# A gated linear attention with routed experts on one core: scaled states on ScalarE, a second load of values, and a shorter routing sequence

## The chip, the core and the metric

The kernel runs on one core of a Trainium2 chip. The core has five engines that work side by side, each through its own list of instructions and in that list's order: TensorE (PE in the profile, with its weight loads shown as PEld), VectorE (DVE), ScalarE (ACT), GpSimd (POOL) and SyncE (SP). SP here only issues DMAs; ACT and POOL issue some as well. The metric is the device time of one execution in microseconds, as the median of several runs. Lower is better.

## What is computed

A decayed linear attention over 4 batches, 8 heads, 768 tokens and head size 48, and behind it a mixture of 8 experts with one expert for each token:

```python
for t in range(S):
    state = alpha[:, :, t, :, None] * state + np.einsum('bhd,bhe->bhde', k[:, :, t], v[:, :, t])
    y[:, :, t] = np.einsum('bhd,bhde->bhe', q[:, :, t], state)
...
        fresh_e = int(np.argmax(logits[b, s]))
        if s == 0 or local_gate[b, s] < 0.5:
            e = fresh_e
        else:
            e = prev_e if prev_e >= 0 else fresh_e
        prev_e = e
...
        h = np.maximum(x[b, s] @ w1[e], 0.0)
        out[b, s] = p[e] * (h @ w2[e])
```

The attention's output of one token (8 heads of 48, that is 384 numbers) is the expert layer's input x. The expert of a token depends on the tokens before it, since a closed local gate takes over the expert of its predecessor. The hidden size of an expert is 1024. Everything is in float32; the expert matmuls split each operand into a high and a low part (`hi`, `lo`) and add three products.

## The kernel before

**The attention loop.** The 3072 tokens are 24 blocks of 128 tokens (`NB`), and block i belongs to batch i % 4, so four independent states take turns. The loop at L684 has 26 passes, called slots here; in slot i the steps of neighbouring blocks are interleaved. From L658 on (`pinned[0] = True`) the program order of each engine is kept, so that order decides who stands behind whom. One slot i issues, in this order:

- `one_a(i+2)` (a small memset on POOL) and `scan2(i+1)`: the backward scan `sf` on DVE, then the product of k with it on POOL.
- `kt(i)`: four transposes on PE into `kp`, copied by ACT to `kk`.
- `copies(i-1)`: two copies on ACT of the states into `sb`. `state(i-1)`: the scaled state with which the batch's next block begins, one operation on DVE.
- `pm(i)`: 32 small matmuls into `pe`, masked by DVE to `pq`.
- up to three of the one-time preparations in `made` (L660), most of them on POOL.
- `other()`, the first of three places a slot. Each place lets every routing sequence go one step, and then either issues matmuls of zeros (`dense`, two a place, so six a slot) or, once the experts have begun, one piece of expert work. The first place of a slot gives no piece before slot 24.
- `scan1(i+2)`: the forward scan `A` and a reciprocal on DVE, then the product of q with `A` on POOL. Loads of block i+3 on SP.
- `xt(i-2)`: three transposes of the finished rows; after each fourth block a routing sequence is added (slots 5, 9, 13, 17, 21 and 25).
- `ym(i-1)`: 48 matmuls into `y`, of which the last 16 read `sb`; ACT copies them to `XR` and stores them to `xd`. A load of values on SP.
- `first_v(i+1)`: ACT copies the first 64 rows of the values beside themselves, since the update wants them in a form of their own.
- the second place; `um(i)`: 16 matmuls into `up`, and DVE adds the state (`st`); the third place.

**The routing.** `route(g)` (L432) finds for four blocks the expert and the place of each token. It is a generator: each `yield` ends a step, and a step is issued at a place. Before, it has 16 steps (13 for the last group): logits `lg`, transposes `lt`, the argmax chain ending in `kr`, an empty step, `rp`, the scan `em`, `rb`, the counts `oi`, the probability, `pw`, the places ending in `oa`, then the value rows `vo` (POOL) and the one-hot rows `on` (ScalarE, two operations for each of the four blocks, spread over four steps; the last group has both on DVE), and eight matmuls `lp` on PE whose sum DVE adds to `acc`. `acc` is the list from which tokens are gathered.

**The early experts.** When the routing of the first 12 blocks ends (`T1`), `work[0] = early()` (L562) begins: it gathers the tokens of expert 0, waits out four more places, and then yields pieces: two transposes (`tp`), eight `h` pieces of the first matrix (`gemm1`, nine matmuls each), eight pieces of the second, then the same for expert 1. The PSUM buffer `tr` is one and is shared by `kp`, `xp` and `tp`; the buffer for all routing results is one as well (`RT`). After the loop, routing 5 is run out place by place, one piece each; then the rest of the experts follow at L738 and L753.

**Start.** Before the order is pinned, POOL clears constants and work buffers (L269 to L280 and L647 to L655), and the first blocks are loaded by `load_a`, `load_x` and `load_v`, nine DMAs on SP's queue.

Of the kernel before, what the change touches and what calls it, by code (L numbers as in the profile page):

```python
# [45 lines left out]
DN0 = 32  # L46
DN = 2
HL = ("h", "h", "up", "pe")
# [18 lines left out]
def gla_moe(ctx, tc, akq, vw, vn, wg, w1, w2, cst, tok, out):  # L67
# [45 lines left out]
    def cc(k, p0=0, p1=128):  # L113
        a, b = _off[k]
        return cs[p0:p1, a:b]
# [140 lines left out]
    with ExitStack() as ac, ExitStack() as aa:  # L256
# [16 lines left out]
        for j in range(2):  # L273
            sb = ap.tile([R, 2, 2, CW], F32, bufs=1, name=f"sb{j}")
            g_.memset(sb[0:64], 0.0)
            g_.memset(sb[64:112, :, 1, :], 0.0)
            SBs.append(sb)
            oh = ap.tile([128, E, G + 1], F32, bufs=1, name=f"oh{j}")
            g_.memset(oh, 0.0)
            OHs.append(oh)  # L280

# [29 lines left out]
        def load_v(i):  # L311
            at = i % G * NBB + i // G
            y_.dma_start(VTs[i % NP][:, 1, :], vn[:, at * DM:(at + 1) * DM])

        def first_v(i):
            vt = VTs[i % NP]
            s_.copy(vt[0:64, 0, :], vt[0:64, 1, :])

        def scan1(i):

            d = blk[i]
            x, a = d["x"], d["a"]
            A = ap.tile([R, SW], F32, tag="A", bufs=3, name=f"A_{i}")
            v_.tensor_tensor_scan(A, a[:, 0:SW], z1, 0.0, ALU.mult, ALU.add)
            d["end"] = A[:, 2 * C + 1:SW:2 * (C + 1)]
            v_.reciprocal(z2[0:R, 2 * C + 1:SW:2 * (C + 1)], d["end"])
            q2 = x[:, BW:].rearrange("p (s t) -> p s t", t=C)
            g_.tensor_tensor(q2, q2, A.rearrange("p (s t) -> p s t", t=C + 1)[:, :, 1:], ALU.mult)
            d["k"] = x[:, 0:BW].rearrange("p (h t) -> p h t", h=HP)
            d["q"] = x[:, BW:2 * BW].rearrange("p (h t) -> p h t", h=HP)  # L330

        def one_a(i):
            a = blk[i]["a"]
            g_.memset(a[:, C + 1:SW:2 * (C + 1)], 1.0)
# [60 lines left out]
        def state(i):  # L395
            d = blk[i]
            if i + G < NB:
                sn = ap.tile([R, 3, HP, D], F32, tag="st", bufs=G + 1, name=f"st_{i + G}")
                v_.scalar_tensor_tensor(sn[:, 0], d["s3"][:, 2], 1.0 / SEED,
                                        d["end"].unsqueeze(2).broadcast_to([R, HP, D]), ALU.mult, ALU.mult)  # L400
                st["S", i % G] = sn
# [30 lines left out]
        def route(g):  # L432
# [4 lines left out]
            def rt(shape, nm, dt=F32, bufs=2):  # L437
                return ap.tile(shape, dt, tag=nm, bufs=bufs, name=f"{nm}_{g}")
# [29 lines left out]
            yield  # L468
            yield

# [27 lines left out]
            v_.reciprocal(se, se)  # L498
            yield
            v_.tensor_tensor(ex, ex, ob, ALU.mult)  # L500
            pn = rt([128, n], "pn")
            v_.tensor_reduce(pn, ex, AX.X, ALU.add)
            v_.tensor_tensor(pl[:, :, 0], pn, se, ALU.mult)
            yield
# [3 lines left out]
            t_.matmul(pw[:, :, 0:n], lhsT=trif, rhs=o4, start=False, stop=True)  # L508
            yield
            ps = rt([128, E, n + 1], "ps")  # L510
            v_.tensor_tensor(ps, pw, st["c"].unsqueeze(2).broadcast_to([128, E, n + 1]), ALU.add)
# [23 lines left out]
            on = ap.tile([128, n, TS], F32, bufs=1, tag="on", name=f"on_{g}")  # L535
            if end:
                v_.tensor_tensor(on, iob.unsqueeze(1).broadcast_to([128, n, TS]),
                                 rr.unsqueeze(2).broadcast_to([128, n, TS]), ALU.is_equal)
            else:
                for j in range(n):  # L540
                    s_.activation(on[:, j], iob, AF.Abs, bias=rr[:, j:j + 1], scale=-1.0)
                    s_.activation(on[:, j], on[:, j], AF.Relu, bias=one[:, 0:1], scale=-float(TS))
                    if j < n - 1:
                        yield
            yield
# [16 lines left out]
        def early():  # L562
# [8 lines left out]
            for _ in jobs[0].gather():  # L571
                yield False
            for _ in range(4):
                yield False
            for _ in jobs[0].trans():
# [45 lines left out]

        def other(pieces=True):

            flush()
            for r in list(steps):
                if next(r, 0) == 0:
                    steps.remove(r)
            if work[0] is None:
                if DN:
                    dense(DN)  # L630
            else:
                if last and drained[0]:
                    last[0].ht, last[0].yt = HL, YL
                for done in work[0] if pieces else ():
                    if done or steps or not drained[0]:
                        break

        work, drained = [None], [False]
        for i in range(3):
# [7 lines left out]
        g_.memset(one, 1.0)  # L647
        g_.memset(m5, 1.0)
        g_.memset(m5[:, :, 0], 0.0)
        for e in range(E):  # L650
            g_.memset(c0[:, e:e + 1], float(e * RS - 1))
            g_.memset(c1[:, e:e + 1], float(e * RS - 1 + (C1 if e in EARLY else 0)))
        g_.tensor_copy(trif, cc("tri"))
        g_.memset(trif[0:64, 64:128], 1.0)
        g_.memset(trif[64:128, 0:64], 0.0)  # L655
        nc.scalar.dma_start(xd[0:1], z2[127:128, 0:DM])
        first_v(0)
        pinned[0] = True  # L658
        dense(DN0)
        made = [  # L660
            lambda: g_.memset(fill, 0.0),
            lambda: g_.tensor_copy(fill.bitcast(I32)[:, 1:2], tk[0:SL, 2 * NB:]),
# [12 lines left out]
                                     -float(SENT), None, ALU.add),  # L675
            lambda: g_.tensor_copy(vals[:, :, 2], tk[:, 1:2 * NB:2]),
        ]
        one_a(0)
        scan1(0)
        scan2(0)  # L680
        one_a(1)
        scan1(1)
        wsteps = iter(())
        for i in range(NB + 2):  # L684
# [16 lines left out]
            other(i >= NB)  # L701
            if i + 2 < NB:
# [238 lines left out]
```

## Time and profile before

| what | value |
|---|---|
| three runs | 488.93, 488.33, 485.93 us; median 488.33 us |
| the profiled execution, its own time | 484.0 us |
| its span, first to last instruction | 482.2 us |
| mean granted TensorE clock over the span | 0.961 |
| HBM read and written | 55.84 MB and 10.62 MB |
| blocks 1 to 22 of the attention loop, from mask `pq` to mask | 20.59 to 153.57 us |

In the profile a row of the groups gives the line, engine, operation, the output and its inputs by the program's names, the shape, the count, then busy microseconds and the mean nanoseconds of one. As a helper records every operation, all have line L81; tiles tell them apart. A row of a timeline begins with its start and its duration in microseconds, and where the engine had been idle before it, the idle time and what ended it stand in brackets. A row of the windows gives the length of a stretch and then the busy time of each engine, the granted clock as a share of full speed, and the DMA engines' share and rate.

### The profile page before, as it was taken

The numbers are of one execution on the slowest core, as the hardware profiler recorded it, in microseconds if no ns is written. First come the engines' busy times: TensorE is split into PE (matmuls) and PEld (weight loads), VectorE is DVE, ScalarE is ACT, GpSimd is POOL, SyncE is SP. The second block draws the span as 40 slices with busy tenths as digits, with TensorE's granted clock in tenths as the row PEclk, the third lists the DMA queues.
The fourth block names the chain that finished last, engine by engine and source line by source line (L and its number), as shares of the span: only waits on it lengthen the run. The fifth ranks groups of instructions, "written<-read, shape, count | busy, mean of one in ns | idle before, by whom it ended". The sixth has DMA issues, their size and how long they took to land.

```text
span 482.2 us, 10873 instructions
## 1 busy us (share of the span) xinstructions
PE 437.9 (91%) x4443; PEld 391.5 (81%) x4443; DVE 257.3 (53%) x485; ACT 194.1 (40%) x390; POOL 186.7 (39%) x207
## 2 busy tenths in 40 slices
PE   5999898999997978698989999999999999999990
PEld 5777776878875877597878998998989989989990
DVE  4778999898997235722274445244254252342310
ACT  1345656565756436321354324335144233242210
POOL 6654326364556000261053642724732503504201
PEclk9799999999998899888899999999999999999997
DMA  8789767596661102660075554444351542531100
GB/s 217 199 260 252 222 187 201 164 292 167 189 208 50 51 17 71 180 186 27 1 224 188 134 181 138 124 131 123 114 175 57 158 130 65 174 98 39 50 3 27
DMA packets 26710, 66.01 MB, mean 137 GB/s; under 512 B 4384, under 2 KB 10677, under 8 KB 26658
## 3 DMA queue, kind: packets, MB, share of 16 engines
q1 hardware_dynamic: 18672, 49.65, 36.3%
q0 software_dynamic: 3840, 10.62, 6.9%
q10 hardware_dynamic: 4146, 5.03, 3.1%
q8 instruction: 35, 0.57, 0.5%
q14 instruction: 17, 0.14, 0.1%
HBM read 55.84 MB, written 10.62 MB: 138 GB/s over the span
## 4 chain that ended last, share of the span: by engine, by line
PE 53%; issue 11%; DVE 9%; ACT 3%; POOL 2%; POOLq 0%; DVEq 0%; ACTq 0%
PE h L81 24%; PE yp L81 20%; PE y L81 3%; PE tp L81 2%; DVE A L81 2%; POOL out L81 1%; PE up L81 1%; DVE st L81 1%; DVE sf L81 1%; DVE pq L81 1%; ACT hh L81 1%; POOL w1l_0b L81 1%; PE pe L81 1%; DVE xl L81 1%; PE lp L81 1%
## 5 line engine op out<-in xcount | busy, mean ns | idle before, releaser
L81 DVE SCALAR_TENSOR_TENSOR hl<-h,hh 128x480 fp32r<-128x480 f32 (+2 forms) x80 | 43.9, 556 | 77.2 <-ACT hh L81 76.9
L81 ACT ACTIVATE hh<-h 128x480 fp32r<-128x480 f32 (+2 forms) x80 | 38.7, 490 | 82.4 <-PE h L81 82.3
L81 POOL DMA_INDIRECT out<-yo,idx x32 | 32.5, 1017 | 80.5 <-DVE yo L81 78.0
L81 POOL DMA_INDIRECT xg<-xd,idx x32 | 32.6, 1018 | 61.0 <-PE tp L81 52.9
L81 DVE TENSOR_SCALAR yo<-yp,acc 128x384 f32<-128x384 f32 (+1 forms) x32 | 19.6, 616 | 61.1 <-PE yp L81 61.0
L81 POOL TENSOR_TENSOR x<-x,sf 112x512 f32<-112x512 f32 x24 | 29.0, 1209 | 42.5 <-DVE sf L81 42.5
L81 POOL TENSOR_TENSOR x<-x,A 112x512 f32<-112x512 f32 x24 | 31.8, 1327 | 29.0 <-DVE A L81 6.6
L81 DVE TENSOR_TENSOR_SCAN A<-a,z 112x520 f32<-112x520 f32 x24 | 34.5, 1437 | 5.6 <-POOL a L81 5.6
L81 PE MATMUL h<-dz 128*128 128x256 f32 x142 | 35.0, 354 | 2.1 <-DVE z L81 2.1
L81 DVE TENSOR_TENSOR_SCAN sf<-a,z 112x520 f32<-112x520 f32 x24 | 33.8, 1408 | 0.1
L81 ACT COPY sb<-st 48x384 f32<-48x384 f32 x48 | 24.5, 510 | 11.5 <-DVE st L81 10.9
L81 PEld LDWEIGHTS h<-dz 128*128 128x128 f32 x142 | 23.8, 224 | 6.5 <-DVE z L81 2.1
L81 PEld LDWEIGHTS y<-vt,pq 64*64 64x64 f32 x768 | 24.9, 138 | 4.0 <-issue 3.8
L81 PE MATMUL y<-vt,pq 64*64 64x48 f32 x768 | 27.9, 224 | 0.0
L81 PE MATMUL y<-sb,x 112*64 112x96 f32 x384 | 21.8, 258 | 4.3 <-ACT sb L81 4.2
L81 PE MATMUL up<-vt,kk 128*48 128x96 f32 (+1 forms) x384 | 23.1, 267 | 0.0
L81 PEld LDWEIGHTS y<-sb,x 112*64 112x64 f32 x384 | 17.2, 140 | 6.2 <-ACT sb L81 5.2
L81 PEld LDWEIGHTS up<-vt,kk 128*48 128x48 f32 (+1 forms) x384 | 18.3, 140 | 3.4 <-issue 1.0
L81 ACT COPY kk<-kp 128x448 f32<-128x448 f32 x24 | 12.8, 531 | 20.7 <-PE kp L81 20.6
L81 PE MATMUL h<-xh,w1h_1a 128*128 128x256 f32 (+1 forms) x48 | 16.4, 342 | 3.9 <-DVE hl L81 2.7
L81 ACT COPY XR<-y 128x384 f32<-128x384 f32 x24 | 11.5, 479 | 20.1 <-PE y L81 20.1
L81 ACT CAST xh<-tp 128x384 fp32r<-128x384 f32 (+1 forms) x32 | 14.0, 462 | 13.9 <-PE tp L81 13.6
(247 smaller groups left out, 1234.8 us busy)
## 6 DMA issues: line engine op xcount, KB each, us to landing
x<-akq SPq DMA_DIRECT2D x24, 448.0 KB, 5.6
a<-akq SPq DMA_DIRECT2D x24, 227.9 KB, 4.5
vt<-vn SPq DMA_DIRECT2D x24, 192.0 KB, 2.7
xd<-XR ACTq DMA_DIRECT2D x24, 192.0 KB, 4.8
rw_0a<-w SPq DMA_DIRECT2D x3, 512.0 KB, 4.9
rw_0a<-w SPq DMA_DIRECT2D x4, 384.0 KB, 4.2
rw_1a<-w SPq DMA_DIRECT2D x3, 512.0 KB, 5.9
rw_1a<-w SPq DMA_DIRECT2D x4, 384.0 KB, 3.5
```

What stands on the lines that cost most here:

```text
L81: r = f(*a, **k)
```

## The change

Nothing changes in the arithmetic's result; what changes is where and when parts are done.

- The next state (`state`) is made by four ScalarE activations with a scale for each partition, in place of one DVE operation. The scale `dec` is made on POOL in `scan1`. In a slot, `kt(i)` now stands behind `copies(i-1)` and `state(i-1)`, so ScalarE copies `kk` after these.
- `first_v` goes; `load_v` issues a second DMA of 96 KB that loads the first 64 rows again.
- `on` is one DVE comparison for all groups. The product of the probability goes from DVE to POOL (`eo`).
- The routing has 11 steps: the empty step and the three in which `on` was spread are gone, two others are joined, so that `vo` and `on` stand at one place and `lp` at the next. `early()` waits out two places, not four.
- Matmuls of zeros: two at a slot's first place, one at each of the others, four a slot.
- POOL clears less ahead of the loop: one-time memsets move into `made`, of which up to five a slot are issued; `c0` and `c1` are worked out by two DVE operations, a copy and two memsets. The first product of q (`scale_q(0)`) stands behind the first `scan2`.

```diff
-DN = 2
+DN = 1
@@ buffers
-            g_.memset(sb[0:64], 0.0)
-            g_.memset(sb[64:112, :, 1, :], 0.0)
+            if j == 0:
+                g_.memset(sb[0:64], 0.0)
+                g_.memset(sb[64:112, :, 1, :], 0.0)
...
-            g_.memset(oh, 0.0)
@@ load_v
             y_.dma_start(VTs[i % NP][:, 1, :], vn[:, at * DM:(at + 1) * DM])
-
-        def first_v(i):
-            vt = VTs[i % NP]
-            s_.copy(vt[0:64, 0, :], vt[0:64, 1, :])
+            y_.dma_start(VTs[i % NP][0:64, 0, :], vn[0:64, at * DM:(at + 1) * DM])
@@ scan1
-            q2 = x[:, BW:].rearrange("p (s t) -> p s t", t=C)
-            g_.tensor_tensor(q2, q2, A.rearrange("p (s t) -> p s t", t=C + 1)[:, :, 1:], ALU.mult)
+            d["A"] = A
+            if i + G < NB:
+                d["dec"] = ap.tile([R, HP], F32, tag="dec", bufs=4, name=f"dec_{i}")
+                g_.tensor_scalar(d["dec"], d["end"], 1.0 / SEED, None, ALU.mult)
+            if i:
+                scale_q(i)
...
+        def scale_q(i):
+            q2 = blk[i]["x"][:, BW:].rearrange("p (s t) -> p s t", t=C)
+            g_.tensor_tensor(q2, q2, blk[i].pop("A").rearrange("p (s t) -> p s t", t=C + 1)[:, :, 1:], ALU.mult)
@@ state
-                v_.scalar_tensor_tensor(sn[:, 0], d["s3"][:, 2], 1.0 / SEED,
-                                        d["end"].unsqueeze(2).broadcast_to([R, HP, D]), ALU.mult, ALU.mult)
+                for hp in range(HP):
+                    s_.activation(sn[:, 0, hp], d["s3"][:, 2, hp], AF.Copy, scale=d["dec"][:, hp:hp + 1])
@@ route
             yield
-            yield
...
-            yield
-            v_.tensor_tensor(ex, ex, ob, ALU.mult)
-            pn = rt([128, n], "pn")
-            v_.tensor_reduce(pn, ex, AX.X, ALU.add)
-            v_.tensor_tensor(pl[:, :, 0], pn, se, ALU.mult)
+            eo = rt([128, n, 8], "eo")
+            g_.tensor_tensor(eo, ex, ob, ALU.mult)
             yield
             pw = pp.tile([128, E, n + 1], F32, tag=RT, name=f"pw_{g}")
...
             yield
+            pn = rt([128, n], "pn")
+            v_.tensor_reduce(pn, eo, AX.X, ALU.add)
+            v_.tensor_tensor(pl[:, :, 0], pn, se, ALU.mult)
...
-            if end:
-                v_.tensor_tensor(on, iob.unsqueeze(1).broadcast_to([128, n, TS]),
-                                 rr.unsqueeze(2).broadcast_to([128, n, TS]), ALU.is_equal)
-            else:
-                for j in range(n):
-                    s_.activation(on[:, j], iob, AF.Abs, bias=rr[:, j:j + 1], scale=-1.0)
-                    s_.activation(on[:, j], on[:, j], AF.Relu, bias=one[:, 0:1], scale=-float(TS))
-                    if j < n - 1:
-                        yield
+            v_.tensor_tensor(on, iob.unsqueeze(1).broadcast_to([128, n, TS]),
+                                              rr.unsqueeze(2).broadcast_to([128, n, TS]), ALU.is_equal)
             yield
@@ early
-            for _ in range(4):
-                yield False
+            yield False
+            yield False
@@ other
-                if DN:
-                    dense(DN)
+                dense(dn)
@@ before the loop
         made = [
+            lambda: g_.memset(SBs[1][0:64], 0.0),
+            lambda: g_.memset(SBs[1][64:112, :, 1, :], 0.0),
+            lambda: g_.memset(one, 1.0),
+            lambda: g_.memset(OHs[0], 0.0),
+            lambda: g_.memset(OHs[1], 0.0),
+            lambda: g_.memset(m5, 1.0),
+            lambda: g_.memset(m5[:, :, 0], 0.0),
+            lambda: g_.tensor_copy(trif, cc("tri")),
...
         one_a(0)
         scan1(0)
         scan2(0)
+        scale_q(0)
@@ a slot
-            if i < NB:
-                kt(i)
             if 0 < i <= NB:
                 copies(i - 1)
                 state(i - 1)
             if i < NB:
+                kt(i)
+            if i < NB:
                 pm(i)
...
-            for _ in range(min(3, len(made))):
+            for _ in range(min(5, len(made))):
                 made.pop(0)()
-            other(i >= NB)
+            other(i >= NB, 2)
...
-            if i + 1 < NB:
-                first_v(i + 1)
```

More of the change, by code (lines that the diff above doesn't have):

```diff
@@ L274, in gla_moe @@
             sb = ap.tile([R, 2, 2, CW], F32, bufs=1, name=f"sb{j}")
-            g_.memset(sb[0:64], 0.0)
-            g_.memset(sb[64:112, :, 1, :], 0.0)
+            if j == 0:
+                g_.memset(sb[0:64], 0.0)
+                g_.memset(sb[64:112, :, 1, :], 0.0)
             SBs.append(sb)
-            oh = ap.tile([128, E, G + 1], F32, bufs=1, name=f"oh{j}")
-            g_.memset(oh, 0.0)
-            OHs.append(oh)
+            OHs.append(ap.tile([128, E, G + 1], F32, bufs=1, name=f"oh{j}"))
         st = {"c": c0}
@@ L620, in gla_moe, with other @@
         last, EW, steps = [], {}, []
-        def other(pieces=True):
+        def other(pieces=True, dn=DN):
             flush()
@@ L646, in gla_moe @@
                 nc.scalar.dma_start(wgs, wg[:, :, 0:32])
[L647 to L655, printed above, removed]
         nc.scalar.dma_start(xd[0:1], z2[127:128, 0:DM])
-        first_v(0)
         pinned[0] = True
@@ L660, in gla_moe @@
         made = [
+            lambda: g_.memset(SBs[1][0:64], 0.0),
[6 more added lines that the diff above has]
+            lambda: g_.tensor_copy(trif, cc("tri")),
+            lambda: g_.memset(trif[0:64, 64:128], 1.0),
+            lambda: g_.memset(trif[64:128, 0:64], 0.0),
             lambda: g_.memset(fill, 0.0),
@@ L676, in gla_moe @@
             lambda: g_.tensor_copy(vals[:, :, 2], tk[:, 1:2 * NB:2]),
+            lambda: v_.tensor_scalar(c0, ioa[:, :, 0], WH, float(TS), ALU.subtract, ALU.mult),
+            lambda: v_.tensor_scalar(c0, c0, -1.0, None, ALU.add),
+            lambda: g_.tensor_copy(c1, c0),
+        ] + [
+            lambda e=e: g_.memset(c1[:, e:e + 1], float(e * RS - 1 + C1)) for e in EARLY
         ]
```

## The prediction

> **What bounds the kernel now.** First the page: the busy shares of the engines.
>
> ```profile
> PE 437.9 (91%) x4443; PEld 391.5 (81%) x4443; DVE 257.3 (53%) x485; ACT 194.1 (40%) x390; POOL 186.7 (39%) x207
> ```
>
> TensorE is busy for 91%, but an average hides the stages. So next the windows, cut at the ends of `up` in slots 5, 11, 15, 19, then at the end of slot 23, at the end of the third `h` piece of expert 1 (208), and the rest (from a second call).
>
> ```profile
> core 0: us, PE busy (x) PEld busy (x) DVE busy (x) ACT busy (x) POOL busy (x), PEclk, DMA share, GB/s
> 22.50:46.50 24.00, 22.33 (x461) 18.66 (x460) 18.38 (x29) 12.54 (x26) 12.81 (x19) 1.00 0.86 249
> 46.50:88.70 42.20, 37.30 (x699) 31.23 (x699) 38.45 (x74) 25.94 (x60) 18.16 (x21) 0.96 0.65 192
> 88.70:113.90 25.20, 24.42 (x477) 20.50 (x477) 22.72 (x48) 15.89 (x40) 12.41 (x13) 1.00 0.78 237
> 113.90:137.00 23.10, 22.73 (x468) 19.26 (x468) 21.78 (x48) 14.75 (x38) 12.62 (x16) 1.00 0.70 193
> 137.00:171.20 34.20, 29.08 (x485) 24.00 (x485) 20.43 (x50) 16.92 (x42) 11.84 (x11) 0.90 0.28 82
> 171.20:208.00 36.80, 28.81 (x234) 25.88 (x235) 20.15 (x59) 15.80 (x35) 6.97 (x7) 0.92 0.38 113
> 250.00:460.00 210.00, 209.20 (x1133) 193.15 (x1132) 82.80 (x128) 73.48 (x118) 82.65 (x57) 1.00 0.41 123
> ```
>
> From 250 on TensorE has no gap (209.20 of 210.00), and the change touches nothing there: what is won or lost earlier is carried to the end. Slots 6 to 11 are bounded by VectorE (38.45 of 42.20, it also splits expert 0's weights), slots 12 to 19 by TensorE (24.42 of 25.20 and 22.73 of 23.10) with VectorE close behind. In the last two stages nobody is full: TensorE idles 5.1 and 8.0 us, and its clock is 0.90 and 0.92, while pieces wait for their places. That idle time is what a shorter routing can win.
>
> **The change part by part.** The sum goes by these stages. First the rows for the loop.
>
> ```profile
> 108.67 0.55 PE L81 MATMUL kp<-cs,x 112*128 112x112 f32 x4
> ...
> 112.58 0.50 PE L81 MATMUL h<-dz 128*128 128x256 f32 x2
> 113.01 0.88 PE L81 MATMUL up<-vt,kk 128*48 128x96 f32 x16
> 113.82 0.51 PE L81 MATMUL h<-dz 128*128 128x256 f32 x2
> 114.17 0.55 PE L81 MATMUL kp<-cs,x 112*128 112x112 f32 x4
> ```
>
> ```profile
> L81 PE MATMUL h<-dz 128*128 128x256 f32 x142 | 35.0, 354 | 2.1 <-DVE z L81 2.1
> L81 DVE SCALAR_TENSOR_TENSOR st<-st,A 112x192 f32<-112x192 f32 x20 | 7.6, 378 | 0.0
> L81 DVE TENSOR_TENSOR on<-iob,rr 128x512 f32<-128x512 f32 x1 | 0.7, 684 | 0.0
> L81 ACT COPY vt<-vt 64x384 f32<-64x384 f32 x24 | 12.3, 512 | 12.3 <-ACT XR L81 8.5 <-DMA vt<-vn 3.9
> L81 ACT ACTIVATE on<-on,one 128x128 f32<-128x128 f32 x20 | 8.0, 402 | 0.6
> L81 ACT COPY L<-lt 128x36 f32<-128x36 f32 x6 | 1.0, 172 | 0.4 <-PE lt L81 0.4
> PE y L81 <- ACT sb L81: 4.2, 7, 1.1
> ```
>
> *Zeros.* A pair takes 0.35 to 0.43 us of TensorE's order (113.82 to 114.17, 112.58 to 113.01), so one takes 0.19. Of 142, 32 stand before the loop and 110 in it; the new loop has four a slot until routing 2 ends in slot 16, that is 67. A slot has two fewer, 0.38 us, which counts only where TensorE is the bound.
>
> *ScalarE.* Four activations of 48 elements with a scale by partition lie between the 0.17 of `L` and the 0.40 of `on`; I take 0.25, nearer to `L`, the smaller shape: 1.0 us a slot, 20 us in all, while 12.3 (`vt`) and two times 8.0 (`on`) go. ScalarE has room (15.89 of 25.20). What counts is order: `sb` comes up to one `kk` copy earlier, which helps `y` (it waited for `sb` 7 times, 4.2 us), and `kk` comes behind both copies and the four activations, so that I let `up` wait 0.5 us in those same slots. I take 0, ends -4 and +4 us. The Trainium skill's page "ScalarE: Activation LUTs", What ACT_TABLE_LOAD costs, gives 280 + 0.833 N ns with a per-partition operand, 0.32 us here as an estimate; by it the four take 1.3 us, and the sum stays.
>
> *VectorE* loses the 0.33 to 0.38 of the state in each slot, and gets 0.68 of `on` a group. `dec`, `eo` and `c1` are a few numbers wide on POOL, as are the two operations for `c0` on VectorE; outside the start they are put at nothing, since POOL is free for half of each stage. *The second load* is one more issue for SP a block, and 96 KB; the values are wanted two slots later, so it is hidden at nothing; without that cover four blocks of it at the 249 GB/s of the busiest stage (DMA 0.86) cost 1.6 us.
>
> *Start to slot 5.*
>
> ```profile
> 6.34 1.24 DVE L81 TENSOR_TENSOR_SCAN A<-a,z 112x520 f32<-112x520 f32 x1 [4.23 <-POOL a L81]
> 11.28 1.24 DVE L81 TENSOR_TENSOR_SCAN A<-a,z 112x520 f32<-112x520 f32 x1 [1.33 <-POOL a L81]
> a<-akq SPq DMA_DIRECT2D x24, 227.9 KB, 4.5
> ```
>
> POOL holds back both first scans. The first can begin when `a` has landed, about 0.7 + 4.5 = 5.2 us: 1.1 us earlier. The second wins less, about 0.8, since q's product (1.2) now stands ahead of the second memset. Then POOL must do the moved memsets in slots 0 to 4, between k's and q's products, with `dec` ahead of the latter; and the memset of `st`, for which VectorE waits in slots 0 to 3, is behind them. I put 0.15 for each `dec` and 0.9 for memsets that find no gap: -0.8 + 0.6 + 0.9 = **+0.7**, ends -1.1 and +2.5.
>
> *Routing.* In a group's last slot, `vo` and `on` now stand at the second place and `lp` at the third.
>
> ```profile
> 93.71 0.88 PE L81 MATMUL up<-vt,kk 128*48 128x96 f32 x16
> 94.38 1.24 DVE L81 TENSOR_TENSOR_SCAN A<-a,z 112x520 f32<-112x520 f32 x1
> 96.19 0.19 DVE L81 TENSOR_TENSOR ps<-pw,ps 128x40 f32<-128x40 f32 x1
> 97.75 0.29 DVE L81 TENSOR_TENSOR oa<-ioa,sl 128x128 f32<-128x128 f32 x1
> 95.75 1.18 POOL L81 TENSOR_TENSOR x<-x,A 112x512 f32<-112x512 f32 x1 [1.79 <-PE kp L81]
> 102.17 2.19 POOL L81 TENSOR_TENSOR x<-x,A 112x512 f32<-112x512 f32 x1
> L81 POOL TENSOR_TENSOR vo<-oa,vals x5: 827/1764/1765, 73.5 to 179.7; 128x384 f32<-128x384 f32 x5
> 200.42 1.10 PE L81 MATMUL lp<-vo,on 128*128 128x96 f32 x8 [2.50 <-DVE on L81]
> ```
>
> POOL takes `vo` only behind q's product, which waits for the scan `A`; the steps `ps` to `oa` (1.85 us from 96.19 to 98.04) now stand ahead of that scan. In slot 12 `A` ended 1.0 us behind `up` (95.62 and 94.59); with the steps ahead of it, but without the state's operation and the probability's product before it, I put it 0.3 behind. Then 0.25 for `dec` and its start, 1.18 for the product, 0.83 for `vo`, and a third of the 0.68 of `on`, since POOL slows beside VectorE (the same product took 1.18 and 2.19, `vo` 0.83 and 1.76): TensorE stands at `lp` for about **2.8 us**, and behind it `kt` and `pm` of the next slot; VectorE stands at `acc`, ahead of its next scan. The nearest row is the one `lp` that follows its `on` at one place's distance now, and it waited 2.50. Ends: 1.5, if TensorE comes late; 4.4, with 2.19 and 1.76 for product and `vo`. This comes in slots 8, 12, 16 and 20; in slot 24 POOL and VectorE are free.
>
> *The clock.*
>
> ```profile
> 150.80:154.21 3.41, 1.90 (x47) 1.49 (x48) 2.04 (x4) 1.42 (x4) 3.25 (x3) 1.00 0.01 2
> 154.21:161.04 6.83, 6.83 (x75) 6.16 (x71) 1.42 (x9) 2.83 (x7) 1.82 (x2) 0.50 0.20 61
> 191.76:195.17 3.41, 2.08 (x13) 1.75 (x14) 2.03 (x6) 2.03 (x4) 1.05 (x1) 1.00 0.76 248
> 198.58:202.00 3.42, 1.58 (x14) 1.61 (x15) 2.97 (x8) 0.00 (x0) 1.05 (x1) 1.00 0.40 158
> 202.00:208.82 6.82, 6.10 (x30) 5.63 (x29) 2.40 (x8) 1.15 (x3) 4.75 (x5) 0.50 0.83 241
> ```
>
> On a grid of 3.41 us, windows in which TensorE idled 1.51 and 1.84 us are followed by 6.8 us at 0.50; after one with 1.33 idle the clock stayed at 1.00. A wait of 2.8 us puts more than 1.4 into one window in every position but the middle. A cut of 6.8 us costs a full TensorE at most 3.4, I take 2.7. Four waits, less where VectorE is the bound anyway: I take two such cuts, **+5.0**, ends 0 and 10.8. The Trainium skill's page "TensorE: Matmul & The Clock Gate", Part 1: The HAM clock gate, has the clock fall after an idle window of about 3.4 us; by that rule waits of 2.8 cut nothing, and the sum below would be -6.8. The rows above speak against it: half a window was enough.
>
> *Early experts.* Routing 2 ends at the third place of slot 16, not at the second of slot 18, and two empty places go; the transposes come in slot 19, not 21 and 22, and at the end of slot 23 eight `h` pieces are done instead of three. After the loop routing 5 needs nine places, not eleven. The two gathers go to slot 17, where they stand in POOL's queue ahead of the next memset and k's product; POOL has 10.5 of 23.1 us free there, so they cost nothing.
>
> ```profile
> 152.31 0.57 PE L81 MATMUL kp<-cs,x 112*128 112x112 f32 x4 [1.86 <-issue]
> 169.84 1.34 PE h L81 x9
> ```
>
> The sum by stages, without the clock's +5.0:
> - slots 6 to 11: VectorE wins 6 x 0.33 = 2.0 and loses about 2.5 at `acc` in slot 8; its 3.75 us of idle time take up the rest: **0**, ends -2 and +2.5.
> - slots 12 to 15: 24.42 - 4 x 0.38 + 2.8 = 25.7 against 25.2: **+0.5**.
> - slots 16 to 19: 22.73, less eleven zeros (2.1), plus 2.8, plus two transposes (1.0) and the wait of what shares their PSUM buffer, twice 1.86: 28.1 against 23.1: **+5.0**.
> - slots 20 to 23: 29.08, less 2.7 that the cut clock cost there and 1.0 of transposes, plus five pieces of 1.34, plus 2.3 at `lp` (a piece stands in between): 34.4 against 34.2: **+0.2**.
> - to the third piece of expert 1: 28.81 less five pieces (6.7) and 2.5 of cut clock is 19.6, and I leave half of the 8.0 us of idle time: 23.6 against 36.8: **-13.2**.
>
> Together 0.7 + 0 + 0.5 + 5.0 + 0.2 - 13.2 = **-6.8 us**.
>
> In all -6.8 + 5.0 = -1.8: the profiled execution, 484.0 us, would go to 482.2, and the median of the runs, which lies 4.3 above it, from 488.3 to **486.5**.
>
> **The rivals.**
> - *Faster: the waits cut no clock.* Then -6.8: 481.5. With waits of 1.5 in place of 2.8 as well, another 5.2: 476.3. For it: zeros still fill the slots, and 1.33 of idle time cut nothing. Against: the rows with 1.51 and 1.84. The Trainium skill's rule quoted above is this case.
> - *Slower: the wait at `lp` is 4.4 us.* POOL's product and `vo` take their long forms (2.19, 1.76), since VectorE's `on` contends: four times 1.6 more, and slot 8 cuts the clock too (2.7): 486.5 + 9.1 = 495.6. It decides from 6.7 us in all, about 1.7 a wait.
> - *The change doesn't do what it says: ScalarE's states hold up `up`.* `kk` behind four activations costs 0.5 us in the slots where `st` comes late, +4: 490.5, seen as no change. For it: the 7 waits of `y` for `sb`. Against: ScalarE's room.
>
> **How the numbers follow.** About 1% (4.9 us) is what a measurement of this kernel tells from no change. Forecast 0.36; faster 0.32; slower 0.24; ScalarE 0.08, of which 0.03 ends beyond 1%. So faster 0.32, same 0.36 + 0.05 = 0.41, slower 0.27. The forecast's own range is 482 to 491; with the others in, 477 to 496, which leaves out the far ends of both.
>
> **What would show it.** `lp` with about 2.5 to 3 us of idle time before it in slots 8, 12, 16 and 20, and half clock right after; the first `h` piece in slot 20, not 22; the stretch from slot 24 to the third piece of expert 1 near 23 us, not 37; 99 matmuls of zeros. Wrong would be: `lp` without waits, or a full clock in slots 12 to 20 (then faster); `up` waiting for `kk` in most slots; or a last stretch of over 30 us, by which the early start would buy nothing.

## The result, and the profile after

The changed kernel takes 532.15 us, the median of four runs (528.15 to 534.56), against 488.19 us for the kernel before on the same chip: 1.090 times, with an interval of 1.081 to 1.099. It is 9% slower; the range on record (477 to 496) misses it by 36 us. Ratios leave out executions over 1.5% above the fastest of their kernel, so one can differ a little from the quotient of the medians; each experiment is compared with runs of the kernel before on its own chip, and the profiles of runs 1, 2, 4 and 6 are of executions that the ratios leave out.

The profiled execution of the changed kernel has a span of 526.3 us, 44.1 more than before, and a mean granted clock of 0.899. From its page, the busy shares, the granted clock in 40 slices, and three groups (count, then busy time and mean ns of one, then idle time ahead of them and what ended it):

```profile
PE 461.3 (88%) x4400; PEld 408.7 (78%) x4400; DVE 248.7 (47%) x466; ACT 187.5 (36%) x406; POOL 188.3 (36%) x220
...
PEclk9776766777989979995889999999999999999997
...
L81 PE MATMUL xp<-cs,XR 128*128 128x128 f32 x72 | 15.3, 331 | 23.3 <-ACT kk L81 22.8
...
L81 PE MATMUL h<-dz 128*128 128x256 f32 x99 | 30.5, 398 | 2.1 <-DVE z L81 2.1
```

The same clock row of the kernel before:

```profile
PEclk9799999999998899888899999999999999999997
```

TensorE is busy for 23.4 us more although 43 matmuls of zeros are gone, and idle for 20.7 us more; together that is the 44.1. The second part has a name in the page: `xp` now waits 22.8 us behind ScalarE's `kk`, where it did not wait before. The first is the clock, which in these traces is granted either in full or at half. From span and mean clock, 2 x (1 - 0.899) x 526.3 = 106 us ran at half clock, against 2 x (1 - 0.961) x 482.2 = 38.

The windows of the changed kernel, cut at the same points as those of before (ends of `up` in slots 1, 5, 11, 15 and 19, end of slot 23, end of the third `h` piece of expert 1; the columns are those shown there):

```profile
23.87:59.76 35.89, 30.98 (x453) 25.28 (x454) 17.25 (x26) 14.43 (x38) 14.78 (x33) 0.71 0.61 175
59.76:118.63 58.87, 48.44 (x687) 39.71 (x686) 35.65 (x68) 26.01 (x69) 16.79 (x27) 0.71 0.49 144
118.63:150.72 32.09, 26.48 (x469) 21.76 (x469) 23.21 (x48) 14.77 (x42) 12.02 (x18) 0.89 0.67 199
150.72:179.25 28.53, 23.39 (x461) 19.23 (x460) 21.70 (x45) 14.50 (x42) 15.22 (x19) 0.94 0.64 184
179.25:220.10 40.85, 34.24 (x532) 29.52 (x533) 18.93 (x48) 14.70 (x38) 9.18 (x10) 0.92 0.23 68
220.10:252.40 32.30, 25.98 (x185) 23.16 (x184) 17.98 (x50) 11.28 (x22) 4.05 (x5) 0.74 0.36 114
```

Stage by stage that is +11.9, +16.7, +6.9, +5.4, +6.7 and -4.5 us, with +1.35 ahead of the first and -0.3 behind the last. The loss lies in all the slots, most in slots 2 to 11 (clock 0.71), and only the stretch behind slot 23 won anything.

One slot shows the mechanism. Slot 14 of the changed kernel ran at full clock, which was granted without a break from 130.0 to 153.9 us; its timeline (start, duration, engine, operation, in square brackets the idle time ahead of it):

```profile
137.45 0.56 DVE L81 TENSOR_TENSOR st<-up,st 112x384 f32<-112x384 f32 x1 [2.34 <-PE up L81]
...
137.63 0.55 PE L81 MATMUL kp<-cs,x 112*128 112x112 f32 x4
...
138.04 1.03 ACT L81 COPY sb<-st 48x384 f32<-48x384 f32 x2
...
138.11 0.69 PE L81 MATMUL pe<-x 48*64 48x64 f32 x32
...
138.74 0.51 PE L81 MATMUL h<-dz 128*128 128x256 f32 x2
138.98 1.00 ACT L81 ACTIVATE st<-st,dec 112x48 f32<-112x48 f32 x4
...
139.90 0.51 ACT L81 COPY kk<-kp 128x448 f32<-128x448 f32 x1
...
140.46 0.55 PE L81 MATMUL xp<-cs,XR 128*128 128x128 f32 x3 [1.22 <-ACT kk L81]
...
143.25 0.88 PE L81 MATMUL up<-vt,kk 128*48 128x96 f32 x16
```

The same slot of the kernel before:

```profile
101.71 0.55 PE L81 MATMUL kp<-cs,x 112*128 112x112 f32 x4
...
102.30 0.53 ACT L81 COPY kk<-kp 128x448 f32<-128x448 f32 x1 [0.24 <-PE kp L81]
...
102.82 0.51 PE L81 MATMUL h<-dz 128*128 128x256 f32 x2
102.86 1.03 ACT L81 COPY sb<-st 48x384 f32<-48x384 f32 x2
...
103.16 0.49 PE L81 MATMUL xp<-cs,XR 128*128 128x128 f32 x3
```

`kp` and `xp` take turns in the one PSUM buffer `tr`, and `kk` is what empties it. Before, ScalarE copied `kk` as soon as `kp` stood there, and the buffer was free before TensorE came to `xp`. Now ScalarE first waits for `st` (0.56), then makes two `sb` (1.03) and four activations (one starts every 0.23, together 1.00), and only then `kk` (0.51): 3.0 us from the end of `up` until `xp` may begin. TensorE has `kp`, `pe` and two zeros for that time, about 1.8 us, and stands 1.22. Since `xp`, `y` and the next `up` follow on TensorE, and the next `st` follows that `up`, this is a ring, and its length comes back in each slot.

### The profile page after: what moved, and what is told of

Same layout as the page of the kernel before. It is cut to its first block, busy times and chain, and to the rows that moved or that the text cites. A ratio compares the mean times of both kernels' runs of the same rounds, so it can differ in the third digit from the quotient of the medians.

```text
span 526.3 us, 10855 instructions
## 1 busy us (share of the span) xinstructions
PE 461.3 (88%) x4400; PEld 408.7 (78%) x4400; DVE 248.7 (47%) x466; ACT 187.5 (36%) x406; POOL 188.3 (36%) x220
## 4 chain that ended last, share of the span: by engine, by line
PE 59%; ACT 11%; issue 10%; DVE 8%; POOL 4%; DMA 4%; ACTq 0%; SPq 0%; POOLq 0%
PE h L81 22%; PE yp L81 18%; PE y L81 10%; ACT sb L81 4%; ACT st L81 3%; PE xp L81 3%; PE up L81 2%; DMA a<-akq 2%; POOL x L81 2%; DVE st L81 2%; ACT kk L81 1%; PE tp L81 1%; DMA rw_1a<-w 1%; POOL out L81 1%; PE lp L81 1%
## 5 line engine op out<-in xcount | busy, mean ns | idle before, releaser
L81 PEld LDWEIGHTS y<-vt,pq 64*64 64x64 f32 x768 | 32.5, 172 | 5.1 <-issue 5.0
L81 PE MATMUL y<-vt,pq 64*64 64x48 f32 x768 | 35.9, 258 | 0.0
L81 PE MATMUL xp<-cs,XR 128*128 128x128 f32 x72 | 15.3, 331 | 23.3 <-ACT kk L81 22.8
L81 PE MATMUL h<-dz 128*128 128x256 f32 x99 | 30.5, 398 | 2.1 <-DVE z L81 2.1
L81 DVE TENSOR_TENSOR st<-up,st 112x384 f32<-112x384 f32 (+1 forms) x24 | 12.5, 519 | 41.3 <-PE up L81 36.0
L81 PEld LDWEIGHTS xp<-cs,XR 128*128 128x128 f32 x72 | 8.9, 160 | 27.3 <-ACT kk L81 26.6
L81 PE MATMUL y<-sb,x 112*64 112x96 f32 x384 | 28.4, 308 | 1.3 <-ACT sb L81 1.3
L81 PE MATMUL up<-vt,kk 128*48 128x96 f32 (+1 forms) x384 | 27.1, 297 | 0.0
L81 PEld LDWEIGHTS y<-sb,x 112*64 112x64 f32 x384 | 22.9, 177 | 3.1 <-ACT sb L81 1.5
L81 PEld LDWEIGHTS h<-dz 128*128 128x128 f32 x99 | 19.5, 245 | 7.3 <-issue 3.0
```

Source lines behind the costliest of these rows:

```text
L81: r = f(*a, **k)
```

## The experiments

Theory: the ring through `kk` costs the time, by its idle time and by the half clock that follows. Rivals: the fewer zeros, the routing's missing places, the new start, the second load, ScalarE's states. The first four runs take parts alone.

**1. Changed kernel, `kt` first again.**

```diff
+            if i < NB:
+                kt(i)
             if 0 < i <= NB:
                 copies(i - 1)
                 state(i - 1)
-            if i < NB:
-                kt(i)
```

> The changed kernel with one thing undone: `kt(i)` stands again ahead of `copies` and `state`, so that `kk` is ScalarE's first copy of a slot; four zeros, ScalarE's states, the second load, the short routing and the new start stay. Theory (ring): the state's four activations and both `sb` copies ahead of `kk` make TensorE wait at `xp` for the shared PSUM buffer, and this idle time cuts the clock; then `xp`'s idle time behind `kk` falls from 22.8 us to under 4, slot 12 begins near 92 us instead of 121, and the time is 480 to 498. Rival (zeros): two fewer zeros a slot let the clock fall; they are unchanged here, so slot 12 still begins past 110 and the time stays over 515. Rival (routing and start): the waits at `lp` or the moved memsets cost the time; over 515 as well, and slot 6 still begins near 60.

505.03 us, 1.025 (1.018 to 1.033). `xp` waits for nothing, and 27 us are back by the medians; but the time lies above the range that the ring theory gave, so something else costs 2.5%. TensorE now waits in the routing. From the waits of this kernel (us in all, times, longest):

```profile
PE pw L81 <- DVE se L81: 5.0, 2, 2.5
...
PE rp L81 <- DVE kr L81: 4.5, 3, 2.4
...
PE lp L81 <- POOL a L81: 4.0, 1, 4.0
```

and the timeline around that `lp`:

```profile
136.79 1.23 DVE L81 TENSOR_TENSOR_SCAN A<-a,z 112x520 f32<-112x520 f32 x1
...
138.11 0.79 POOL L81 TENSOR_SCALAR dec<-A 112x4 f32<-112x4 f32 x1 [2.65 <-DVE A L81]
...
138.87 1.17 POOL L81 TENSOR_TENSOR x<-x,A 112x512 f32<-112x512 f32 x1
...
140.00 0.83 POOL L81 TENSOR_TENSOR vo<-oa,vals 128x384 f32<-128x384 f32 x1
...
140.88 2.02 PE L81 MATMUL lp<-vo,on 128*128 128x96 f32 x8 [4.01 <-POOL a L81]
```

This is the predicted chain, scan, `dec`, product, `vo`, `lp` (the view names a small memset of POOL that ended beside `vo`). It came once, at 4.0 us; the other waits came at places that the prediction did not name.

**2. Kernel before, `kt` behind copies and state.** The edit of 1 reversed, in the kernel before.

> The kernel before with one thing changed: `kt(i)` behind `copies` and `state`; the state stays one operation on VectorE. From the end of `up` to `xp` the ring is then `st` 0.56, two `sb` 1.04, `kk` 0.50, about 2.1 us instead of 3.1 with four activations; TensorE has `kp`, `pe` and two zeros, about 1.8 us, to fill it. Theory (ring, activations decide): `xp` waits 0.2 to 0.4 us a slot, 4 to 9 us in all, few cuts of the clock: 488 to 503. Rival (order alone decides): `xp` waits 20 us or more as in the changed kernel, and the time is over 515. Rival (zeros or routing): no change, 486 to 491.

506.96 us, 1.038 (1.030 to 1.047), and in its waits:

```profile
PE xp L81 <- ACT kk L81: 12.3, 18, 2.4
```

The order alone costs 3.8%, with all six zeros and the old routing. The wait and the time lie above what the theory gave, and below what its rival asked for. The ring is a cause, even without activations in it.

**3. Kernel before, four zeros a slot.** `dense(2)` at the first place, `dense(1)` at the others.

> The kernel before with four zeros a slot instead of six (two at the first place, one at each of the others); nothing else. Theory (ring): the zeros are no cause by themselves; TensorE has 0.38 us less in slots where it is the bound, and one or two more cuts of the clock at most: 484 to 494. Rival (zeros): without the two zeros the clock falls in slots 1 to 12 as in the changed kernel, granted mean under 0.93, and the time is over 510.

488.62 us, 0.990 (0.984 to 0.997), runs from 479.70 to 496.81. The spread is wide, but even the longest run is only 2% above the kernel before (median 487.28): the zeros are not the cause of the 9%.

**4. Changed kernel, six zeros a slot.** `DN = 2`.

> The changed kernel with six zeros a slot instead of four (two at each place); nothing else. Theory (ring): the two more stand behind `y` and behind `up`, not ahead of `xp`; the ring gets 0.2 to 0.4 us longer, `xp` still waits over 18 us for `kk`, the clock still falls: 515 to 545. Rival (zeros): the clock stays full in slots 1 to 12 and the time comes to under 500.

525.95 us, 1.078 (1.072 to 1.084); `xp` still waits 20.2 us for `kk`. Two more zeros win 1% at most (the interval touches that of the changed kernel) and mend nothing.

**5. As 1, the routing at sixteen places.**

```diff
@@ behind kr, and ahead of pw
+            yield
@@ ahead of lp
+            yield
+            yield
+            yield
@@ early
-            yield False
-            yield False
+            for _ in range(4):
+                yield False
```

> The kernel of the first experiment (changed kernel, `kt` first) with the routing's steps at sixteen places again: the empty places behind `kr`, ahead of `pw` and ahead of `lp` (three), and four instead of two behind the gathers; the instructions of each step stay those of the change. In the first experiment TensorE stood 2.5 us at `pw` in slots 7 and 11, 4.0 at `lp` in slot 15 and 2.8 at the transposes in slot 19, and half clock followed each time. Theory (two causes: the ring through `kk`, and the routing's missing places): these four waits go to under 1 us each, and the time is 480 to 492. Rival (ScalarE's states, the second load or the start cost what is left): the time stays at 497 to 508.

494.34 us, 1.019 (1.010 to 1.029). The waits at `pw` and `lp` are gone, and yet the ratio is hardly under that of 1, and the time is above the range expected; the intervals overlap. In this kernel something else costs the 2%.

**6. Changed kernel, the state on VectorE.**

```diff
-                for hp in range(HP):
-                    s_.activation(sn[:, 0, hp], d["s3"][:, 2, hp], AF.Copy, scale=d["dec"][:, hp:hp + 1])
+                v_.scalar_tensor_tensor(sn[:, 0], d["s3"][:, 2], 1.0 / SEED,
+                                        d["end"].unsqueeze(2).broadcast_to([R, HP, D]), ALU.mult, ALU.mult)
```

> The changed kernel with the state as one operation on VectorE again (`dec` is still computed and not read); `kt` stays behind copies and state. Theory (ring): without the four activations (0.95 us) the ring from `up` to `xp` is about 2.1 us instead of 3.1; `xp`'s idle time behind `kk` falls from 22.8 to 8 to 14 us, and the time from 530 to 505 to 522 (the order alone made the kernel before 3.8% slower, the routing's places cost some more). Rival (the order alone is the ring's whole cost): `xp` still waits over 20 us and the time stays at 525 or more.

516.88 us, 1.058 (1.044 to 1.071); `xp` idles 10.3 us behind `kk`. The ring, one microsecond shorter, costs less, as expected.

**7. As 1, with two empty places, ahead of `pw` and of `lp`.**

> The kernel of the first experiment with two empty places put back, one ahead of `pw` and one ahead of `lp` (thirteen places). Theory (two causes): the waits at `pw` and `lp` go, the early experts still start sooner than before, and the time is 478 to 492, at least 8 us below the first experiment. Rival (what is left lies in ScalarE's states, the load or the start): 497 to 508.

496.07 us, 1.025 (1.016 to 1.033): no better than 1 as a ratio, and against the expectation. `lp` no longer waits, but `lg` of the next group now waits 7.3 us for `acc`.

So 2% were still unexplained without the ring. Runs 8 to 10 cross the old start with six zeros.

**8. As 5, with the old start**, the memsets ahead of the loop as before.

> The changed kernel with `kt` first, the routing at sixteen places, and the start of the kernel before (its memsets ahead of the loop, q's product of block 0 inside the first scan); four zeros a slot. In the same kernel with the new start TensorE idled 3.12 us in slot 0 and then ran 17 us at half clock. Theory (the new start is the next cost): slot 6 begins near 47 us instead of 50.2, and the ratio to the kernel before comes from 1.02 to 0.99 to 1.01. Rival (ScalarE's states or the second load cost what is left): the ratio stays at 1.015 to 1.03. Rival (few zeros make the cuts long): still cuts of over 10 us, 1.00 to 1.02, with a wide spread of the runs.

496.29 us, 1.022 (1.011 to 1.033). The ratio stays, as the first rival had it.

**9. As 5, with six zeros.**

> The changed kernel with `kt` first, the routing at sixteen places and six zeros a slot; the new start stays. Theory (few zeros make the cuts long): no cut of over 10 us after slot 5, ratio 0.995 to 1.015. Theory (the start): the idle time in slot 0 and the cut at 16 us stay, ratio 1.01 to 1.02. Rival (ScalarE's states or the second load): 1.02 to 1.03.

492.40 us, 1.016 (1.006 to 1.025). Two more zeros do not move it clearly either.

**10. As 5, with old start and six zeros.** That is the kernel before with the state on ScalarE, the second load, and `on` and `eo` in one operation each.

> The kernel before with three parts of the change only: the state on ScalarE (with `dec`), the second load in place of the copy, and `on` and `eo` in one operation each, at the old places; `kt` first, old start, six zeros. Theory (ring, missing places, start and zeros made the loss): nothing of it is here, 0.985 to 1.005. Rival (ScalarE's states or the second load cost 2%): 1.015 to 1.03.

496.57 us, 1.025 (1.015 to 1.035). My theory that start and zeros made the rest falls: neither moves the ratio beyond the intervals. The 2% lie in what 10 still has. (In runs 5 and 8 to 10 the last routing has sixteen places too, where it had thirteen before; behind the last `up`, run 10 takes 313.7 us and the kernel before 313.1, so that is not it.) Two more runs part it.

**11. As 10, `on` on ScalarE again**, as pairs of activations in four steps.

> The kernel of the tenth experiment (kernel before with the state on ScalarE, the second load, and `eo`) with `on` on ScalarE again, as pairs of activations at four places. In the tenth, `on` as one comparison took 1.31 us on VectorE beside POOL's `vo`, ahead of the scan `A`: behind it `st` and `sb` came late in slots 10 and 13, and `xl` in slot 21, where TensorE stood 5.6 us instead of 1.9. Theory (`on` on VectorE is what is left): these waits go back to those of the kernel before, and the ratio is 0.98 to 1.005. Rival (ScalarE's states or the second load): 1.015 to 1.03, and TensorE still stands over 4 us in slot 21.

483.37 us, 0.998 (0.993 to 1.003). ScalarE's states, the second load and `eo` together cost nothing that can be measured.

**12. Kernel before, `on` on VectorE.**

```diff
-                for j in range(n):
-                    s_.activation(on[:, j], iob, AF.Abs, bias=rr[:, j:j + 1], scale=-1.0)
-                    s_.activation(on[:, j], on[:, j], AF.Relu, bias=one[:, 0:1], scale=-float(TS))
...
+            v_.tensor_tensor(on, iob.unsqueeze(1).broadcast_to([128, n, TS]),
+                                              rr.unsqueeze(2).broadcast_to([128, n, TS]), ALU.is_equal)
+            for _ in range(0 if end else 3):
+                yield
```

> The kernel before with one part of the change alone: `on` as one comparison on VectorE, ahead of three empty places. Theory (`on` on VectorE is what is left): 1.01 to 1.03, TensorE stands over 4 us in slot 21. Rival (ScalarE's states or the second load): 0.99 to 1.005.

489.23 us, 1.016 (1.010 to 1.022): this one operation, in five of the six routings (the last had it on VectorE already), is most of the rest of run 10. From its timeline in slot 21:

```profile
149.51 1.18 POOL L81 TENSOR_TENSOR x<-x,sf 112x512 f32<-112x512 f32 x1 [2.29 <-DVE sf L81]
...
149.93 1.31 DVE L81 TENSOR_TENSOR on<-iob,rr 128x512 f32<-128x512 f32 x1
...
150.13 0.49 PE L81 MATMUL tp<-cs,xg 128*128 128x128 f32 x3
150.65 1.28 POOL L81 TENSOR_TENSOR vo<-oa,vals 128x384 f32<-128x384 f32 x1
151.16 1.86 DVE L81 TENSOR_TENSOR_SCAN A<-a,z 112x520 f32<-112x520 f32 x1
...
153.40 2.03 DVE L81 TENSOR_TENSOR_SCAN sf<-a,z 112x520 f32<-112x520 f32 x1
...
155.35 0.53 DVE L81 TENSOR_TENSOR xl<-tp,xh 128x384 fp32r<-128x384 f32 x1
...
155.98 0.98 PE L81 MATMUL kp<-cs,x 112*128 112x112 f32 x4 [5.35 <-issue]
```

`on` takes 1.31 us here beside POOL's product of k and `vo`, not 0.68, and stands ahead of both scans and of `xl`, which empties `tr`; TensorE's next `kp` has 5.35 us of idle time ahead of it, against 1.86 in the kernel before. It is the same buffer once more.

The long `on` belongs to sixteen places, though. Of the six in a kernel (shortest, median and longest in ns; this run first, then the changed kernel):

```profile
L81 DVE TENSOR_TENSOR on<-iob,rr x6: 681/1074/1311, 72.3 to 205.8; 128x512 f32<-128x512 f32 x6
...
L81 DVE TENSOR_TENSOR on<-iob,rr x6: 664/674/685, 90.7 to 247.1; 128x512 f32<-128x512 f32 x6
```

In the changed kernel, and likewise in run 1, no `on` took over 0.69 us. So the 2.5% of run 1 are not the long `on`; there the waits at `pw`, `rp` and `lp` (13.5 us in all) stand in its place. Eleven places with `on` on ScalarE were not run, so for the changed routing the two are not parted.

**13. Changed kernel with `kt` first, sixteen places, `on` on ScalarE.** ScalarE's states, the second load, `eo`, the new start and four zeros stay.

> The changed kernel with three things undone: `kt` first, the routing at sixteen places, `on` on ScalarE in four places. The state on ScalarE, the second load, `eo`, the new start and four zeros stay. Theory (ring through `kk`, `on` on VectorE, missing places; nothing else costs): the ratio to the kernel before is 0.985 to 1.01. Rival (four zeros or the new start cost in themselves): 1.015 or more.

485.58 us, 0.996 (0.991 to 1.002). What this kernel keeps of the change costs nothing that can be measured.

**14. As 13, `kt` behind copies and state.**

> The kernel of the thirteenth experiment with `kt` behind copies and state again: the ring through `kk` alone, with the four activations in it. Theory (the ring is the largest part, larger than the 1.038 that the order alone cost with the state on VectorE and six zeros): 1.045 to 1.07, `xp` behind `kk` idle 18 us or more. Rival (the ring costs only together with the missing places): under 1.03.

533.57 us, 1.100 (1.085 to 1.115), more than expected. The group of `xp` in this kernel:

```profile
L81 PE MATMUL xp<-cs,XR 128*128 128x128 f32 x72 | 14.8, 320 | 23.2 <-ACT kk L81 23.2
```

The ring alone gives the whole loss of the changed kernel. Runs 13 and 14 issue the same 4407 matmuls, so they also part the two ways in which it costs: in the profiles TensorE's idle time rises from 48.5 to 62.3 us, and its busy time from 436.0 to 468.2, with a mean clock of 0.958 and 0.894. The slower clock is the larger part.

The parts do not add up: with the ring, `on` and the routing cost nothing on top. VectorE idles 4.7 us a slot in slots 2 to 5 of the changed kernel and 3.9 in slots 6 to 11 (windows above), where it idled 1.4 and 0.6 before; that `on` and the routing find room there is argued, not tested.

**15. A try for a faster kernel: the kernel before, what was put off goes ahead of `sf`.**

```diff
+            if work[0] is not None:
+                flush()
             if i + 1 < NB:
                 scan2(i + 1)
             flush()
```

> A try for a faster kernel: the kernel before, where, from the slot in which the early experts begin, what was put off to VectorE (`xl` and `hl`) goes ahead of the scan `sf` instead of behind it. In slots 21 and 22 TensorE waited 1.86 us at `kp` for `xl` of the shared PSUM buffer, behind two scans, and 6.8 us of half clock followed. Theory: that wait falls under 1 us and that cut goes: 0.985 to 0.997. Rival (the cut comes elsewhere, or `sf` comes late and holds up k's product): 0.997 to 1.01.

480.94 us, 0.994 (0.988 to 0.9996). In its timeline `xl` is now ahead of the scan, and `kp` waits 1.21 us in place of 1.86, not under 1 as expected:

```profile
151.04 0.56 DVE L81 TENSOR_TENSOR xl<-tp,xh 128x384 fp32r<-128x384 f32 x1 [0.50 <-ACT xh L81]
151.52 1.43 DVE L81 TENSOR_TENSOR_SCAN sf<-a,z 112x520 f32<-112x520 f32 x1
...
151.70 0.57 PE L81 MATMUL kp<-cs,x 112*128 112x112 f32 x4 [1.21 <-POOL vo L81]
```

The half clock at 154 us did not come in this profile. The gain is at the edge of what can be measured.

**16. As 11, with the edit of 15.**

> The eleventh experiment's kernel (state on ScalarE, second load, `eo`; else the kernel before) with the same edit as the fifteenth. Theory: as there, 0.98 to 0.995. Rival: 0.995 to 1.01.

485.26 us, 1.004 (0.999 to 1.009): no gain here, so that of 15 is not safe either.

**17. As 13, `kt` between `copies` and `state`.** `kk` is behind `sb` and ahead of the activations.

> The thirteenth experiment's kernel with `kt` between `copies` and `state`: `kk` is behind both `sb` copies, but ahead of the four activations. From the end of `up` to `xp` it is about 2.1 us as in the second experiment. Theory (the length of the ring decides): `xp` idles 8 to 14 us behind `kk`, ratio 1.02 to 1.045, well under the 1.100 with the activations in the ring. Rival (only the order of `kk` and `sb` matters): 1.08 or more.

508.16 us, 1.047 (1.031 to 1.062), a little over the expected range; `xp` idles 13.4 us behind `kk`, against 23.2 in 14. Both copies in the ring cost 5%, the four activations another 5%.

**18. As 14, with `xt(i-2)` issued ahead of copies, state and `kt`.** `kk` is as late as in 14, but `xp` has the buffer first.

> The fourteenth experiment's kernel (`kt` behind copies and state, ratio 1.100) with `xt(i-2)` issued ahead of them in the slot, so that `xp` takes the shared PSUM buffer before `kp` does and no longer waits for `kk`; `kk` itself comes as late as there. Theory (the loss is the wait for the shared buffer): `xp` waits under 3 us in all, `kp` a little for `xx`, ratio 0.99 to 1.04. Rival (the loss is `up`, which waits for the late `kk`): `up` takes over the wait, ratio 1.07 or more.

498.22 us, 1.030 (1.016 to 1.043). `up` waits for nothing here, and `xp` 2.2 us in all. `kp` now waits for `xx`, the copy that takes the transposed rows out of the buffer, 0.6 us in most slots (the view puts it down to "issue"), and has the largest share of the idle time that is left in the loop. A slot of its timeline, and the group of `kp`:

```profile
115.13 0.48 ACT L81 COPY xx<-xp 128x384 f32<-128x384 f32 x1
115.63 1.03 ACT L81 COPY sb<-st 48x384 f32<-48x384 f32 x2
...
115.71 0.57 PE L81 MATMUL kp<-cs,x 112*128 112x112 f32 x4 [0.61 <-issue]
...
116.57 1.01 ACT L81 ACTIVATE st<-st,dec 112x48 f32<-112x48 f32 x4
...
117.48 0.51 ACT L81 COPY kk<-kp 128x448 f32<-128x448 f32 x1
```

```profile
L81 PE MATMUL kp<-cs,x 112*128 112x112 f32 x96 | 15.5, 289 | 17.3 <-issue 9.5 <-POOL x L81 3.5 <-POOL a L81 2.5
```

Of the 10% of 14, 7 went with the wait of `xp` for the shared buffer, with `kk` later still: it starts 3.5 us behind the end of `up` (median of slots 2 to 19), against 2.8 in 14. That the buffer, and not the reader of `kk`, makes most of the loss is shown by this. The 3% that stay were not followed up; the waits of `kp` for the same buffer are the nearest candidate.

## Why the prediction was wrong

**The step that failed** is the term for ScalarE: "I take 0, ends -4 and +4 us." Runs 13 and 14 measure it at 0.104 of the time, about 50 us. The prediction had the right order ("`kk` comes behind both copies and the four activations") and asked only who reads `kk`: `up`, which comes late and indeed waited for nothing, in the changed kernel as in run 18. It did not ask who waits for the PSUM buffer that `kk` empties, though `kp` and `xp` share `tr`, and though it priced a wait for this very buffer elsewhere (twice 1.86 us, for the early transposes). In the changed kernel `xp` waited 22.8 us for it, in 19 slots. It argued from ScalarE's room, a share of busy time; the room was there, the place in the queue was not. The rival with the right name ("ScalarE's states hold up `up`") had the wrong reader, a price of 4 us and a chance of 0.08.

The duration of one activation was a smaller miss: 322 ns, where 0.25 was taken. That the four take 1.0 us a slot, as put, is luck: one starts every 0.23 us, while the one ahead is still running. Here the Trainium skill's page "ScalarE: Activation LUTs" (What ACT_TABLE_LOAD costs), quoted in the prediction with 0.32 us, agrees with the trace for one activation. The 1.3 us that the prediction worked out from it for four does not: they took 1.00. The sum would not have changed by it.

**The clock** was the second term, "+5.0", two cuts of 6.8 us. That idle time in part of a window can cut the clock was right, and the slower clock makes over half of the loss (runs 13 and 14: 32.2 us of busy time against 13.8 of idle time); number and length were wrong. Time at half clock rose from 38 to 106 us, and a cut lasted up to 17 us in the changed kernel.

**VectorE and `on`**: "gets 0.68 of `on` a group", and a third of that at `lp` for contention. In the changed kernel the 0.68 was right. At sixteen places it takes up to 1.31 beside POOL's work, stands ahead of two scans and `xl`, and costs 1.6% alone, some 8 us (run 12); the prediction asked how long it takes, not what stands behind it. What it costs at eleven places is open.

**Routing.** The wait at `lp` was put at 2.8 us in four slots. In the changed kernel `lp` waited 0.3 us for POOL and 1.5 for `on`, and TensorE comes late there anyway; without the ring (run 1) the chain came as described, once, at 4.0, and further waits stood at `pw` and `rp`, the other neighbours of removed places, which the sum did not have. Their price by themselves stays open: runs 1 and 5 differ by less than their intervals.

**Early experts**, "-13.2": all eight `h` pieces were done by the end of slot 23, as predicted, and the stretch behind it shrank from 36.8 to 32.3 us only. The sum left 4.0 us of idle time there and no half clock. TensorE idled 6.3 of the 32.3 us, 4.7 of them at routing 5's `rp`, `rb` and `pw`, behind which the pieces stand, and its clock was 0.74.

**Right** were the zeros (99; by run 3 no loss), the second load and ScalarE's states outside the ring (run 11), and the start: `up` of slot 1 ended 1.35 us later in place of the 0.7, and run 8 shows no gain from taking it back.

## What to carry to other kernels

When an instruction moves back in its engine's queue, list two kinds of waiters: who reads what it writes, and who needs the buffer that it empties. The second kind can sit on another engine and belong to other work. And a wait of one microsecond a slot on the engine that bounds the loop is not one microsecond: here the slower clock behind it cost more than the idle time itself.

## What was not expected of the hardware

Half clock can last while TensorE hardly rests. In run 5 one window, with its columns as above, reads:

```profile
80.70:111.40 30.70, 30.25 (x342) 25.59 (x340) 20.93 (x43) 13.06 (x36) 11.92 (x15) 0.50 0.57 162
```

TensorE was busy for 30.25 of 30.70 us, and the clock stayed at 0.50. The Trainium skill's page "TensorE: Matmul & The Clock Gate" (Part 1: The HAM clock gate) has the full clock back after about 3.4 us of sustained work; this window speaks against it. What ended such stretches was not tested.

The idle time that cuts the clock can be small, too. In the changed kernel:

```profile
150.49:153.90 3.41, 2.58 (x50) 2.05 (x47) 2.96 (x7) 2.35 (x7) 1.18 (x1) 1.00 0.85 274
153.90:157.30 3.40, 3.40 (x47) 2.98 (x49) 3.04 (x10) 0.48 (x1) 0.93 (x2) 0.50 0.13 40
```

Here 0.83 us of idle time was followed by half clock, while in the kernel before 1.33 us was not (prediction). So the idle time of the window just before does not decide by itself; what else does, stays open.
